# Linear attention and a highway layer on one core: a new order for the first chunk, with batch 1's query scaled on GpSimd

## The chip, the core and the metric

The kernel runs on one core of a Trainium2 chip. A core has five engines that work side by side, each with its own queue of instructions in program order: PE (matrix products, with its weight loads shown apart as PEld), DVE (VectorE), ACT (ScalarE), POOL (GpSimd) and SP, which here only issues the DMAs. Engines wait for each other by semaphores. Matrix products go to PSUM, which has eight banks of 128 x 512 numbers of 4 bytes; the rest lives in SBUF, 128 partitions wide. The metric is the time of one execution in microseconds on the device; lower is better.

## The reference

Eight batches, eight heads, 576 rows of 64. Every head computes a linear attention, and a highway layer with two 512 x 512 weights follows:

```
q_s = exp(q) / sum over d of exp(q)
k_s = exp(k) / sum over rows of exp(k)
kv  = k_s^T v                    (64 x 64 for each head)
x   = q_s kv, the heads side by side: 4608 x 512
H   = max(x w_h, 0)
T   = 1 / (1 + exp(-(x w_t + b_t)))
out = T H + (1 - T) x
```

(The reference subtracts maxima before the exponentials; they cancel.) Inputs and output are in 32 bits. The kernel works in 16 bits inside, sums products in 32, and uses T H + (1 - T) x = x + T (H - x), with T from a tanh: T = (1 + tanh(z / 2)) / 2.

## The kernel before

**Layout.** A batch is loaded by three DMAs of 1152 KB (`load`, L84). Two heads share the 128 partitions, and each partition holds nine consecutive rows (index n) of four head pairs (index c). "Half a" of a batch is the two head pairs 2a and 2a+1. The load pool `ld` has three buffers for each of q, k and v; the two weights borrow one buffer of q and one of k (`load_weight`, L99). All DMAs are issued by SP, in program order.

**One batch**, by function:

- `exp_half` (L150): ACT takes the exponential of half of q or k, 32 bits to 16, 128x1152. Tiles `eq` and `ek`.
- `cast_v` (L160): half of v to 16 bits with a column of ones beside it, on POOL unless another engine is given.
- `q_sums` (L195, L199): DVE sums each row of 64 exponentials of a half (tile `r`), and `q_recip` (L204) takes the reciprocals of the batch.
- The query is scaled in place, in two parts (n from 0 to 4 and from 4 to 9): on DVE by `q_scale_v` (a small copy L210 and a product L212 each), or on POOL by `q_scale_p` (L216). Batches 0 and 1 use DVE, the others POOL.
- `q_trans` (L218): PE transposes the scaled query in three groups (4, 4 and 1 rows n) into PSUM (tile `pq`, L64), and DVE copies each to SBUF (tile `qsT`, L233).
- `kv_half` (L167): 36 small products k^T v of half a batch into the two `psk` banks; `kv_norm` (L183): DVE divides by the sums of k that the ones column gave (tiles `rz`, `kvn`).
- `x_pair` (L235): x, transposed, for half a batch and eight of the nine rows n, from `kvn` and `qsT`; three of the four results of a batch are copied to `xT` by ACT (L255), the last by DVE (L257). `x_left` (L259) does the ninth row (tile `x`, L270).

**The highway layer** works by chunks: chunk c is batch c's x without the ninth rows (chunks 8 and 9 are the ninth rows of all batches), and each has four output blocks ob of 128 columns. `gate(c, ob)` (L286) is four matmuls with w_t and a tanh on ACT in place in PSUM (tile `pt`, L291). `carry(c, ob)` (L294) is four matmuls with w_h (tile `ph`) and on DVE `dd` = max(ph, 0) - x (L300). `blend(c, ob)` (L305) is `g` = (tanh + 1) dd on DVE (L308). `out_tile` turns x and g back by matmuls (tile `nat`), and the result is stored.

**PSUM** is dealt to three pools: `ps_ht` with four banks (gates, carries and the warm-up tile), `ps_q` with three (`pq`, `psk`, `px`, `px_l`), `ps_nat` with one. A pool gives a new tile the free bank that was released longest ago, and its first writer waits until the readers of the old tile are done. A gate's bank is released by its blend, a carry's by its dd, the two `psk` banks by `kv_norm`.

**The order** is written out by hand, because the scheduler is switched off (L57). Each engine's queue is the order in which the code emits that engine's instructions. The list at L441 to L468 holds the head: all of batch 0's attention, chunk 0 of the highway layer, batch 1's attention, and the first steps of batch 2. Idle time of PE is filled there with `warm_up` matmuls whose result nobody reads. After it, events at slots p (L380) follow: chunk c has slots 8c to 8c+7, a gate and a carry in turn, and a blend two slots after its gate. A table (L426 to L430) puts batch b's transpositions, kv halves and x_pairs at offsets from slot p = 8(b - 1); `kv_norm` stands right behind the second kv half. For batch 2 the offsets are transpositions 4, 5, 5, kv halves 3, 4, x 6, 7, 7. Within a slot of this table the transpositions are emitted ahead of the kv half.

Loads of the head: q, k, v of batch 0 in halves, the bias, then q of batch 1, w_t, w_h, k of batch 1, v of batch 1 in halves. The loads of batches 2 and 3 stand in the head's list, later ones at slot 8(b - 3).

Of the kernel before, what the change touches and what calls it, by code (L numbers as in the profile page):

```python
# [18 lines left out]
def kernel(  # L19
# [19 lines left out]
    def heads_view(t, b):  # L39
        return t[b].rearrange("(c x) (p n) d -> (x p) c (n d)", x=2, n=N9)  # L40

    pool = lambda name, bufs, **kw: ctx.enter_context(tc.tile_pool(name=name, bufs=bufs, **kw))
    consts = pool("consts", 1)
    ld = pool("ld", 3)
    ekp = pool("ekp", 2)
    eqp = pool("eqp", 2)
    small = pool("small", 2)
# [1 line left out]
    xtp = pool("xtp", 3)  # L49
    gp = pool("gp", 2)  # L50
    mo = pool("mo", 3)
    og = pool("og", 3)
    ps_ht = pool("ps_ht", 4, space=PSUM)
    ps_q = pool("ps_q", 3, space=PSUM)
    ps_nat = pool("ps_nat", 1, space=PSUM)
# [3 lines left out]
    mm = lambda o, l, r, st, sp: nc.tensor.matmul(  # L59
        o, l, r, start=st, stop=sp, skip_group_check=True  # L60
    )
# [6 lines left out]

    ident = consts.tile([P, P], FP16, name="ident")
    half_i = consts.tile([P, P], FP16, name="half_i")  # L70
    w16 = {n: consts.tile([P, 4, 512], FP16, name=f"w16{n}") for n in "ht"}
    brow = consts.tile([4, P], FP32, name="brow")
    id4 = consts.tile([4, 4], FP32, name="id4")
    bt2 = consts.tile([P, 4], FP32, name="bt2")
    kvn = [consts.tile([P, 2, 2, 64], FP16, name=f"kvn{i}") for i in range(2)]
    v16s = [consts.tile([P, N9, 4, 66], FP16, name=f"v16_{i}") for i in range(2)]
    x9 = consts.tile([P, 4, B, 64], FP16, name="x9")
# [35 lines left out]
    for w in "qkv":  # L113
        load(0, w, [nc.sync, nc.sync])
    nc.sync.dma_start(brow, moe_b_t.rearrange("(k p) -> k p", p=P))
    load(1, "q")
    load_weight("t", moe_w_t, "q32")
    load_weight("h", moe_w_h, "k32")
    load(1, "k")
    load(1, "v", [nc.sync, nc.sync])  # L120
# [18 lines left out]
    wide = consts.tile([P, 512], FP16, name="wide")  # L139
    nc.vector.memset(wide, 0.0)  # L140

    def warm_up(n):
        for _ in range(n):
            mm(warm, ident, wide, True, True)


    ek, eq, psk, qsT = {}, {}, {}, {}
    xT, gT = {}, {}

    def exp_half(b, which, a):  # L150
        dst, p_ = {"k": (ek, ekp), "q": (eq, eqp)}[which]
        if a == 0:
            dst[b] = p_.tile([P, N9, 4, 64], FP16, tag="e", name=f"e{which}_{b}")
        nc.scalar.activation(  # L154
# [3 lines left out]
        )  # L158

    def cast_v(b, a, eng=None):  # L160
        (eng or nc.gpsimd).tensor_copy(  # L161
            v16s[b % 2][:, :, 2 * a : 2 * a + 2, 0:64],
            in32["v"][b][:, 2 * a : 2 * a + 2].rearrange("p c n d -> p n c d"),
        )


    def kv_half(b, a):  # L167
# [25 lines left out]
    qsum = {}  # L193

    def q_sums(b, a):  # L195
        if a == 0:
            qsum[b] = small.tile([P, N9, 4], FP32, tag="r32", name=f"r32_{b}")
        h = slice(2 * a, 2 * a + 2)
        nc.vector.reduce_sum(qsum[b][:, :, h], eq[b][:, :, h, :], axis=AX.X)  # L199

    NG = [(0, 4), (4, 8), (8, 9)]

# [70 lines left out]
    rows_of = lambda c: 8 if c < B else 4  # L273

    def views(c):
        if c >= B:
            h = slice(4 * (c - B), 4 * (c - B) + 4)
            return lambda k_: x9[:, k_, h], lambda k_: g9[:, k_, h]
        g, b2 = c // 2, c % 2
        if g not in gT:  # L280
            gT[g] = gp.tile([P, 4, NM, 2, 64], FP16, tag="g", name=f"g_{g}")
        return lambda k_: xT[g][:, k_, :, b2, :], lambda k_: gT[g][:, k_, :, b2, :]

    live = {}

    def gate(c, ob):  # L286
        xv = views(c)[0]
        ps = ps_ht.tile([P, rows_of(c), 64], FP32, tag="ht", name=f"pt_{c}_{ob}")
        for k_ in range(4):
            mm(ps, w16["t"][:, k_, ob * P : ob * P + P], xv(k_), k_ == 0, k_ == 3)  # L290
        nc.scalar.activation(ps, ps, AF.Tanh, bias=bt2[:, ob : ob + 1], scale=0.5)  # L291
        live[c, ob] = ps
# [101 lines left out]
    for g in range(B // 2):  # L394
        p = 16 * (g + 1)
# [6 lines left out]
    p = 8 * B + 8  # L402
# [5 lines left out]
    at(9, E(exp_half, 2, "k", 0), E(q_scale_p, 2, 4, N9))  # L408
    at(10, E(exp_half, 2, "k", 1))
    at(11, E(cast_v, 2, 1, nc.vector))  # L410
    for b in range(2, B):
        p = 8 * (b - 1)
        if b > 2:
            s = p + {3: -2, 4: -4}.get(b, -5)
            at(s, E(exp_half, b, "q", 0))
            at(s + 1, E(exp_half, b, "q", 1), E(q_sums, b, 0))
            at(s + 2, E(q_sums, b, 1), E(q_recip, b))
            if b > 3:
                at(s + 2, E(q_scale_p, b, 0, 4))
# [10 lines left out]
        }.get(b, ((2, 3, 4), (3, 4), (5, 6, 7)))  # L430
# [10 lines left out]
    for f in [  # L441
        E(warm_up, 20),
        E(exp_half, 0, "q", 0), E(q_sums, 0, 0),
        E(exp_half, 0, "q", 1), E(q_sums, 0, 1),
        E(q_recip, 0), E(q_scale_v, 0, 0, 4), E(q_scale_v, 0, 4, N9),
        E(exp_half, 0, "k", 0), E(cast_v, 0, 0),
        E(exp_half, 0, "k", 1), E(cast_v, 0, 1),
        E(q_trans, 0, 0), E(q_trans, 0, 1), E(warm_up, 2), E(q_trans, 0, 2),
        E(warm_up, 6),
        E(kv_half, 0, 0), E(gate_bias), E(warm_up, 2), E(kv_half, 0, 1), E(kv_norm, 0),  # L450
        E(warm_up, 4),
        E(x_pair, 0, 0), E(warm_up, 2), E(x_pair, 0, 1), E(warm_up, 2), E(x_left, 0),
        E(warm_up, 14),
        E(exp_half, 1, "q", 0), E(exp_half, 1, "q", 1),
        E(q_sums, 1, 0),
        *[E(cast_weight, "t", k_, nc.vector) for k_ in range(4)],
        E(q_sums, 1, 1), E(q_recip, 1), E(q_scale_v, 1, 0, 4), E(q_scale_v, 1, 4, N9),
        *[E(cast_weight, "h", k_, (nc.gpsimd, nc.scalar)[k_ % 2]) for k_ in range(4)],
        E(gate, 0, 0), E(gate, 0, 1), E(exp_half, 1, "k", 0), E(cast_v, 1, 0),
        E(carry, 0, 0), E(blend, 0, 0), E(carry, 0, 1), E(blend, 0, 1),  # L460
        E(exp_half, 1, "k", 1), E(cast_v, 1, 1),
        E(q_trans, 1, 0), E(q_trans, 1, 1), E(q_trans, 1, 2),
        E(gate, 0, 2), E(carry, 0, 2), E(blend, 0, 2),
        E(kv_half, 1, 0), E(gate, 0, 3), E(kv_half, 1, 1), E(kv_norm, 1),
        E(carry, 0, 3), *[E(load, b, w) for b in (2, 3) for w in "qkv"],
        E(exp_half, 2, "q", 0),
        E(x_pair, 1, 0), E(x_pair, 1, 1), E(blend, 0, 3), E(x_left, 1),
        E(exp_half, 2, "q", 1), E(q_sums, 2, 0),  # L468
    ]:
        f()  # L470
    for p in range(8, 8 * (B + 2) + 1):
# [33 lines left out]
```

The softmax here doesn't subtract the row's maximum and nothing guards it: scores larger than these inputs give would overflow.

## Time and profile before

| What | Value |
|---|---|
| median of 4 runs (lowest, highest) | 140.39 us (140.24, 140.57) |
| the profiled execution | 140.24 us |
| its span, first to last instruction | 138.2 us |
| granted PE clock, mean | 0.996 |
| busy: PE, PEld | 122.4 us (89%), 69.4 us (50%) |
| busy: DVE, ACT, POOL | 107.1 us (78%), 88.6 us (64%), 44.3 us (32%) |
| DMA | 40.07 MB, mean 290 GB/s |

The profile's second part cuts the span into 40 slices of 3.455 us; a digit is the busy share in tenths:

```
PE   4979999967978799969979999899899999999950
DVE  1395289987998799996998789988987766688860
ACT  3650376819931998639978969769793645565430
POOL 2006003410393619039409800980394000000000
DMA  4999999999999999943999999970043007066774
```

PE's busy time counts the warm-up matmuls of the first 21 us, and matmuls are pipelined, so a 9 is not PE at its best. The DMA engines are full up to about 58 us. Of the chain of work that ended last, PE has 50% of the span, DVE 31%, ACT and POOL 5% each, DMA 3%. Some moments of the head: ACT starts on batch 0's query at 4.41 us, batch 0's products x end near 18, chunk 0's first dd starts at 24.94, batch 1's first x_pair at 31.82, the gate of slot 8 at 34.17, batch 2's first x_pair at 44.37.

A row of the timeline reads: start, duration (both in us), engine, line, operation, output and inputs, shapes, count; in brackets the idle time of that engine just before and what ended it.

### The profile page before, as it was taken

The numbers are of one execution on the slowest core, as the hardware profiler recorded it, in microseconds if no ns is written. First come the engines' busy times: TensorE is split into PE (matmuls) and PEld (weight loads), VectorE is DVE, ScalarE is ACT, GpSimd is POOL, SyncE is SP. The second block draws the span as 40 slices with busy tenths as digits, with TensorE's granted clock in tenths as the row PEclk, the third lists the DMA queues.
The fourth block names the chain that finished last, engine by engine and source line by source line (L and its number), as shares of the span: only waits on it lengthen the run. The fifth ranks groups of instructions, "written<-read, shape, count | busy, mean of one in ns | idle before, by whom it ended". The sixth has DMA issues, their size and how long they took to land.

```text
span 138.2 us, 3619 instructions
## 1 busy us (share of the span) xinstructions
PE 122.4 (89%) x1509; PEld 69.4 (50%) x1509; DVE 107.1 (78%) x208; ACT 88.6 (64%) x130; POOL 44.3 (32%) x37
## 2 busy tenths in 40 slices
PE   4979999967978799969979999899899999999950
PEld 1335344532443355526634654465366455699930
DVE  1395289987998799996998789988987766688860
ACT  3650376819931998639978969769793645565430
POOL 2006003410393619039409800980394000000000
PEclk9999999999999999999999999999999999999998
DMA  4999999999999999943999999970043007066774
GB/s 140 375 386 411 401 389 413 409 413 403 414 414 398 413 409 410 406 176 152 277 409 408 319 312 406 397 294 0 5 175 130 5 0 304 0 251 277 292 267 136
DMA packets 15783, 40.07 MB, mean 290 GB/s; under 512 B 660, under 2 KB 1176, under 8 KB 14744
## 3 DMA queue, kind: packets, MB, share of 16 engines
q1 hardware_dynamic: 15768, 39.85, 75.1%
q8 instruction: 12, 0.20, 0.5%
q14 instruction: 3, 0.02, 0.1%
HBM read 30.41 MB, written 9.44 MB: 288 GB/s over the span
## 4 chain that ended last, share of the span: by engine, by line
PE 50%; DVE 31%; ACT 5%; POOL 5%; issue 3%; DMA 3%; DVEq 0%; POOLq 0%
PE pt L59 14%; DVE r L199 13%; PE ph L59 13%; PE nat L59 9%; POOL eq L216 5%; PE pq L64 4%; DVE g L308 4%; PE psk L59 3%; DVE dd L300 3%; PE warm L59 3%; DMA q<-in_q_dram 3%; ACT eq L154 2%; DVE eq L212 2%; PE px L59 2%; DVE r L204 2%
## 5 line engine op out<-in xcount | busy, mean ns | idle before, releaser
L291 ACT ACTIVATE pt<-pt,bt 128x512 f32<-128x512 f32 (+1 forms) x40 | 24.8, 622 | 27.4 <-PE pt L59 27.4
L59 PE MATMUL pt<-xT,w16t 128*128 128x512 f16 x128 | 33.3, 380 | 2.2 <-DVE xT L257 1.7
L216 POOL TENSOR_TENSOR eq<-eq,r 128x1024 f16<-128x1024 f16 (+1 forms) x12 | 25.6, 2152 | 29.5 <-DVE r L204 29.5
L59 PE MATMUL ph<-xT,w16h 128*128 128x512 f16 x128 | 32.8, 380 | 0.0
L300 DVE SCALAR_TENSOR_TENSOR dd<-ph,xT 128x512 f16<-128x512 f32 x32 | 21.8, 682 | 7.5 <-PE ph L59 7.5
L308 DVE SCALAR_TENSOR_TENSOR g<-pt,dd 128x512 f16<-128x512 f32 (+1 forms) x40 | 25.2, 630 | 2.4
L199 DVE TENSOR_REDUCE r<-eq 128x18 f32<-128x1152 f16 x16 | 21.4, 1344 | 4.2 <-ACT eq L154 4.2
L161 POOL CAST v<-v 128x1152 f16<-128x1152 f32 x15 | 16.9, 1147 | 22.9 <-DMA v<-in_v_dram 20.7
L154 ACT ACTIVATE eq<-q 128x1152 f16<-128x1152 f32 x16 | 18.5, 1172 | 2.6 <-DMA q<-in_q_dram 2.6
L59 PEld LDWEIGHTS <-w16t 128*128 128x128 f16 x160 | 14.0, 97 | 12.3 <-issue 1.1
L59 PE MATMUL nat<-half_i,g 128*128 128x128 f16 x142 | 19.8, 219 | 0.1
L154 ACT ACTIVATE ek<-k 128x1152 f16<-128x1152 f32 x16 | 18.4, 1169 | 1.9 <-DMA k<-in_k_dram 1.9
L59 PEld LDWEIGHTS <-w16h 128*128 128x128 f16 x160 | 13.8, 98 | 10.9 <-issue 1.4
L339 ACT COPY o<-nat 128x512 f32<-128x512 f32 x28 | 16.6, 593 | 2.8 <-PE nat L59 2.0
L59 PE MATMUL nat<-ident,xT 128*128 128x128 f16 x128 | 17.7, 219 | 0.0
L255 ACT CAST xT<-px 128x512 f16<-128x512 f32 x24 | 13.3, 592 | 6.5 <-PE px L59 6.4
L59 PE MATMUL warm<-wide,ident 128*128 128x512 f16 x52 | 15.2, 441 | 1.9 <-DVE wide L140 1.9
L59 PEld LDWEIGHTS <-g 128*128 128x128 f16 x144 | 14.0, 98 | 3.5 <-DVE g L308 0.6
L233 DVE COPY qsT<-pq 128x1024 f16<-128x1024 f16 (+1 forms) x24 | 12.8, 553 | 3.2 <-PE pq L64 3.0
L59 PEld LDWEIGHTS <-xT 128*128 128x128 f16 x128 | 12.5, 98 | 5.0 <-issue 2.6
L64 PE MATMUL pq<-ident,eq 128*128 128x128 f16 x144 | 11.5, 220 | 2.5 <-POOL eq L216 1.4
L64 PEld LDWEIGHTS <-eq 128*128 128x128 f16 x144 | 8.9, 98 | 6.4 <-POOL eq L216 3.1
(43 smaller groups left out, 86.4 us busy)
## 6 DMA issues: line engine op xcount, KB each, us to landing
out_dram<-o SPq DMA_DIRECT2D x8, 1024.0 KB, 4.6
q<-in_q_dram SPq DMA_DIRECT2D x7, 1152.0 KB, 13.8
k<-in_k_dram SPq DMA_DIRECT2D x7, 1152.0 KB, 14.8
v<-in_v_dram SPq DMA_DIRECT2D x6, 1152.0 KB, 14.7
v<-in_v_dram SPq DMA_DIRECT2D x4, 576.0 KB, 10.7
q<-in_q_dram SPq DMA_DIRECT2D x2, 576.0 KB, 4.1
k<-in_k_dram SPq DMA_DIRECT2D x2, 576.0 KB, 6.8
w32t<-in_moe_w_t_dram SPq DMA_DIRECT2D x1, 1024.0 KB, 13.2
```

Source lines behind the costliest of these rows:

```text
L59: mm = lambda o, l, r, st, sp: nc.tensor.matmul(o, l, r, start=st, stop=sp, skip_group_check=True)
L64: nc.tensor.matmul(o, i, ident, is_transpose=True, start=True, stop=True, skip_group_check=True,)
L154: nc.scalar.activation(dst[b][:, :, 2 * a : 2 * a + 2, :], in32[which][b][:, 2 * a : 2 * a + 2].rearrange("p c n d -> p n c d"), AF.Exp,)
L161: (eng or nc.gpsimd).tensor_copy(v16s[b % 2][:, :, 2 * a : 2 * a + 2, 0:64], in32["v"][b][:, 2 * a : 2 * a + 2].rearrange("p c n d -> p n ...
L199: nc.vector.reduce_sum(qsum[b][:, :, h], eq[b][:, :, h, :], axis=AX.X)
L216: nc.gpsimd.tensor_mul(e, e, r.broadcast_to(list(e.shape)))
L233: nc.vector.tensor_copy(qsT[b][:, :, n0:n1, :], t[:, :, 0:w, :])
L255: nc.scalar.copy(dst, t[c])
L291: nc.scalar.activation(ps, ps, AF.Tanh, bias=bt2[:, ob : ob + 1], scale=0.5)
L300: nc.vector.scalar_tensor_tensor(dd, ps, 0.0, xv(ob), op0=ALU.max, op1=ALU.subtract)
L308: nc.vector.scalar_tensor_tensor(gv(ob), th, 1.0, dd, op0=ALU.add, op1=ALU.mult)
L339: nc.scalar.copy(o, flat(t))
```

## The change

- Loads: w_t moves ahead of batch 1's query. Batch 2's v is loaded in two halves. The load of batches 2 and 3 stands at another place of the list.
- w_t's four casts stand ahead of batch 0's x_pair and go to DVE and POOL in turn, instead of four on DVE behind it. w_h's casts stay on POOL and ACT in turn.
- The fourteen warm-up matmuls behind batch 0's products go, and one more; five are put behind the third gate of chunk 0, in a bank of `ps_q`.
- Chunk 0's gates are computed before the carries: (0,0) and (0,1) in `ps_ht`, (0,2) in a bank of `ps_q`, and (0,3) in the bank of `ps_nat`, behind the second carry.
- Batch 1's query: ACT does its second half behind the tanh of gate (0,0); the sums are made by two additions and a reduction of a quarter of the length (`q_sums_tree`); the scaling is on POOL (`q_scale_p`) instead of DVE (`q_scale_v`), behind w_h's casts there.
- Batch 1's v: the first half is cast by ACT, the second as two single head pairs by POOL and ACT.
- Batch 1's transpositions, kv halves and the last blend of chunk 0 are put in another order; both exponentials of batch 2's query stand behind all of batch 1's x products.
- Batch 2's kv halves move from slots p+3 and p+4 to p+4 and p+5, `kv_norm` with the second.
- In SBUF a pad of 128 bytes, the load pool and the output pool now lie ahead of the constants.

```diff
+    pool("pad", 1).tile([P, PAD // 4], FP32, name="pad")
+    ld = pool("ld", 3)
+    og = pool("og", 3)
     consts = pool("consts", 1)
-    ld = pool("ld", 3)
...
+    load_weight("t", moe_w_t, "q32")
     load(1, "q")
-    load_weight("t", moe_w_t, "q32")
     load_weight("h", moe_w_h, "k32")
...
+    def warm_mid(n):
+        t = ps_q.tile([P, 512], FP32, tag="qx", name="warm_mid")
+        for _ in range(n):
+            mm(t, ident, wide, True, True)
...
+    def cast_v_head(b, c, eng):
+        o = v16s[b % 2][:, :, c, 0:64]
+        i = in32["v"][b][:, c]
+        if eng is nc.scalar:
+            eng.copy(o, i)
+        else:
+            eng.tensor_copy(o, i)
...
+    def q_sums_tree(b, a):
+        if a == 0:
+            qsum[b] = small.tile([P, N9, 4], FP32, tag="r32", name=f"r32_{b}")
+        h = slice(2 * a, 2 * a + 2)
+        e = eq[b][:, :, h, :]
+        nc.vector.tensor_add(t32, e[:, :, :, 0:32], e[:, :, :, 32:64])
+        nc.vector.tensor_add(t16, t32[:, :, :, 0:16], t32[:, :, :, 16:32])
+        nc.vector.reduce_sum(qsum[b][:, :, h], t16, axis=AX.X)
...
-    def gate(c, ob):
+    def gate(c, ob, home=None):
         xv = views(c)[0]
-        ps = ps_ht.tile([P, rows_of(c), 64], FP32, tag="ht", name=f"pt_{c}_{ob}")
+        ps, tag = home or (ps_ht, "ht")
+        ps = ps.tile([P, rows_of(c), 64], FP32, tag=tag, name=f"pt_{c}_{ob}")
...
-            2: ((4, 5, 5), (3, 4), (6, 7, 7)),
+            2: ((4, 5, 5), (4, 5), (6, 7, 7)),
...
+        *[E(cast_weight, "t", k_, (nc.vector, nc.gpsimd)[k_ % 2]) for k_ in range(4)],
         E(warm_up, 4),
-        E(x_pair, 0, 0), E(warm_up, 2), E(x_pair, 0, 1), E(warm_up, 2), E(x_left, 0),
-        E(warm_up, 14),
-        E(exp_half, 1, "q", 0), E(exp_half, 1, "q", 1),
-        E(q_sums, 1, 0),
-        *[E(cast_weight, "t", k_, nc.vector) for k_ in range(4)],
-        E(q_sums, 1, 1), E(q_recip, 1), E(q_scale_v, 1, 0, 4), E(q_scale_v, 1, 4, N9),
+        E(x_pair, 0, 0), E(warm_up, 2), E(x_pair, 0, 1), E(warm_up, 1), E(x_left, 0),
+        E(exp_half, 1, "q", 0), E(q_sums_tree, 1, 0),
+        E(gate, 0, 0), E(exp_half, 1, "q", 1), E(q_sums_tree, 1, 1), E(q_recip, 1),
         *[E(cast_weight, "h", k_, (nc.gpsimd, nc.scalar)[k_ % 2]) for k_ in range(4)],
-        E(gate, 0, 0), E(gate, 0, 1), E(exp_half, 1, "k", 0), E(cast_v, 1, 0),
-        E(carry, 0, 0), E(blend, 0, 0), E(carry, 0, 1), E(blend, 0, 1),
-        E(exp_half, 1, "k", 1), E(cast_v, 1, 1),
-        E(q_trans, 1, 0), E(q_trans, 1, 1), E(q_trans, 1, 2),
-        E(gate, 0, 2), E(carry, 0, 2), E(blend, 0, 2),
-        E(kv_half, 1, 0), E(gate, 0, 3), E(kv_half, 1, 1), E(kv_norm, 1),
-        E(carry, 0, 3), *[E(load, b, w) for b in (2, 3) for w in "qkv"],
-        E(exp_half, 2, "q", 0),
-        E(x_pair, 1, 0), E(x_pair, 1, 1), E(blend, 0, 3), E(x_left, 1),
-        E(exp_half, 2, "q", 1), E(q_sums, 2, 0),
+        E(q_scale_p, 1, 0, 4), E(q_scale_p, 1, 4, N9),
+        E(gate, 0, 1), E(gate, 0, 2, (ps_q, "qx")), E(warm_mid, 5),
+        E(carry, 0, 0), E(blend, 0, 0), E(carry, 0, 1), E(exp_half, 1, "k", 0),
+        E(gate, 0, 3, (ps_nat, "nat")), E(blend, 0, 1), E(carry, 0, 2),
+        E(q_trans, 1, 0), E(carry, 0, 3), E(blend, 0, 2),
+        E(exp_half, 1, "k", 1), E(cast_v, 1, 0, nc.scalar),
+        E(cast_v_head, 1, 2, nc.gpsimd), E(cast_v_head, 1, 3, nc.scalar),
+        E(q_trans, 1, 1), E(kv_half, 1, 0), E(q_trans, 1, 2), E(kv_half, 1, 1),
+        E(kv_norm, 1), E(blend, 0, 3),
+        *[E(load, 2, w) for w in "qk"], E(load, 2, "v", [nc.sync, nc.sync]),
+        *[E(load, 3, w) for w in "qkv"],
+        E(x_pair, 1, 0), E(x_pair, 1, 1), E(x_left, 1),
+        E(exp_half, 2, "q", 0), E(exp_half, 2, "q", 1), E(q_sums, 2, 0),
```

More of the change, by code (lines that the diff above doesn't have):

```diff
@@ L32 @@
     P = 128
+    PAD = 128
     N9 = S // 64
@@ L51 @@
     mo = pool("mo", 3)
-    og = pool("og", 3)
     ps_ht = pool("ps_ht", 4, space=PSUM)
@@ L160, in cast_v @@
     def cast_v(b, a, eng=None):
[L161 to L164, printed above, removed]
+        o = v16s[b % 2][:, :, 2 * a : 2 * a + 2, 0:64]
+        i = in32["v"][b][:, 2 * a : 2 * a + 2].rearrange("p c n d -> p n c d")
+        if eng is nc.scalar:
+            eng.copy(o, i)
+        else:
+            (eng or nc.gpsimd).tensor_copy(o, i)
+    def cast_v_head(b, c, eng):
+        o = v16s[b % 2][:, :, c, 0:64]
+        i = in32["v"][b][:, c]
+        if eng is nc.scalar:
+            eng.copy(o, i)
+        else:
+            eng.tensor_copy(o, i)
     def kv_half(b, a):
@@ L199, in q_sums @@
         nc.vector.reduce_sum(qsum[b][:, :, h], eq[b][:, :, h, :], axis=AX.X)
+    t32 = consts.tile([P, N9, 2, 32], FP16, name="t32")
+    t16 = consts.tile([P, N9, 2, 16], FP16, name="t16")
+    def q_sums_tree(b, a):
[6 more added lines that the diff above has]
+        nc.vector.reduce_sum(qsum[b][:, :, h], t16, axis=AX.X)
     NG = [(0, 4), (4, 8), (8, 9)]
```

## The prediction

> **What bounds the kernel now.** The profiled execution took 140.24 us, of which 138.2 are the span and 2.04 lie around it; the median shown is 140.39, 0.15 more. I work in span times and add 2.04. The table of stretches came first: does an early gain survive to the end?
>
> ```profile
> 34.20:47.30 13.10, 10.77 (x141) 5.11 (x138) 11.76 (x23) 7.75 (x11) 8.02 (x5) 1.00 1.04 409
> 47.30:62.00 14.70, 13.06 (x170) 7.00 (x167) 13.98 (x25) 11.19 (x16) 5.32 (x3) 1.00 0.92 359
> 74.20:87.00 12.80, 12.66 (x173) 7.12 (x172) 10.81 (x21) 10.79 (x16) 5.59 (x5) 1.00 0.99 358
> 112.00:121.00 9.00, 9.00 (x76) 5.58 (x75) 5.68 (x10) 5.18 (x10) 0.00 (x0) 1.00 0.28 117
> ```
>
> Columns: stretch, length, busy time of PE, weight load, DVE, ACT, POOL, granted clock, DMA share, GB/s. From 47.3 DVE is nearly full (13.98 of 14.70), from 74 PE is (12.66 of 12.80), and the code there is untouched. Loads do not bind there: SP issues batch 5's three loads between 41 and 47 us, and between 59 and 66 us the DMA row falls to 4 and 3 tenths. So whatever is won or lost by the first half of batch 2's products (x_pair, 44.37 us) reaches the end one for one. The whole question is when that instruction runs.
>
> Ahead of it I read the timeline for the arrivals, which no edit can pull forward:
>
> ```profile
> 21.44 1.14 ACT L109 CAST w16h<-w32h 128x512 f16<-128x512 f32 x2 [1.66 <-DMA w32h<-in_moe_w_h_dram]
> 21.47 1.17 POOL L111 CAST w16h<-w32h 128x512 f16<-128x512 f32 x2 [7.96 <-DMA w32h<-in_moe_w_h_dram]
> 24.25 2.22 ACT L154 ACTIVATE ek<-k 128x1152 f16<-128x1152 f32 x2 [0.53 <-DMA k<-in_k_dram]
> 27.16 1.15 POOL L161 CAST v<-v 128x1152 f16<-128x1152 f32 x1 [0.27 <-DMA v<-in_v_dram]
> 35.88 1.15 POOL L161 CAST v<-v 128x1152 f16<-128x1152 f32 x1 [7.57 <-DMA v<-in_v_dram]
> ```
>
> Bracketed: idle time and what ended it. w_h's cast, batch 1's k and v, and batch 2's v wait on memory while DMA runs at 1.04 and 409 to 412 GB/s. DVE, though, is late at the first carry, and the batch 2 query later waits for POOL:
>
> ```profile
> 24.20 0.82 DVE L212 TENSOR_TENSOR eq<-eq,r 128x1280 f16<-128x1280 f16 x1
> 24.94 0.68 DVE L300 SCALAR_TENSOR_TENSOR dd<-ph,xT 128x512 f16<-128x512 f32 x1
> 25.73 0.69 DVE L308 SCALAR_TENSOR_TENSOR g<-pt,dd 128x512 f16<-128x512 f32 x1
> ...
> 38.15 4.64 POOL L216 TENSOR_TENSOR eq<-eq,r 128x1024 f16<-128x1024 f16 x2 [1.12 <-DVE r L204]
> 38.60 1.02 PE L59 MATMUL pt<-xT,w16t 128*128 128x512 f16 x4 [0.40 <-DVE dd L300]
> 42.84 0.56 PEld L64 LDWEIGHTS <-eq 128*128 128x128 f16 x10 [1.10 <-POOL eq L216]
> ```
>
> The first carry's sum (ready on PE near 23.6) waits behind DVE's scaling of q1 until 24.94. The 38.60 row also shows how banks are handed on: gate (1,2) waits for a dd, the reader of the bank released longest ago. I use that order below.
>
> **The change, step by step.**
>
> *Landings.* Issue start plus time to landing: q1 4.20+11.0=15.2, w_t 4.63+13.2=17.83, w_h 5.77+15.6=21.37. Swapped, w_t lands 2.63 after v0 (cast starts 12.37): 15.0, and q1 at 17.8, where ACT is free anyway (17.66). w_h trails by 3.54 although w_t, of equal size, took 2.63; k1 (2.81) and q2 (2.84), larger, took less too. I take 20.6, near the usual spacing; bounds 20.46 and 21.37.
>
> *Removed.* Fourteen warm-up matmuls (17.9 to 21) and one more; the gates (0,0) to (0,2) and five matmuls take their place. Cost nothing: the clock stayed 1.00 across PE's own holes in 24.94 to 31.8 (5.46 busy of 6.86). w_t's casts: two on DVE (0.36 apart) between 15.40 and x_pair's copy at 17.11, two on POOL (0.59 each): hidden; a landing past 16.4 would push that copy.
>
> *q1's sums.* Per half two adds and a short reduction for one reduction of 1.34. From the fp16 products (1024: 0.69, 1280: 0.825, so 0.52 ns an element) the adds of 576 and 288 cost 0.46 and 0.31; the reduction of 288 lies between 0.16 (DVE's smallest row) and 1.34, at its rate 0.44. With two waits of 0.1: 1.4, no gain. Exponentials at 17.9 and 19.6 with a tanh between, sums to 22.2, reciprocal to 22.6.
>
> *q1's scaling to POOL.* Leaves DVE (0.18+0.69+0.18+0.83); POOL's rows for the same shapes are 1.90 and 2.40, together 4.30 (4.18 to 4.64 pair by pair): 22.75 to 27.05. Its second transposition is then ready at 27.7; DVE reaches its copy at 27.9 (below). Cover 0.2; past it each POOL microsecond is on the path. [...]
>
> *First chunk.* In the trace w_h's landing to the end of both casts is 1.27 (21.37 to 22.64); the last two matmuls with weights (0.10+0.22+0.22) and their fill bring dd to landing plus 2.07: 22.67 instead of 24.94. From there DVE is back to back: a dd to its own blend 0.79, other steps 0.61, a large copy 0.60. dd 22.67, g 23.46, dd 24.07, g 24.86, dd 25.47, query copy 26.07, dd 26.67, g 27.28, query copy 27.88 to 28.57. All four gates are done before that, in banks of the three PSUM pools; the tanh behind the w_h casts on ACT (to 23.7) are early enough for these g.
>
> The third, short transposition gets the bank of the second (two are held by kv): PE 28.62, ready 28.90. The second kv half stands behind it and needs v: ACT does k's exponentials (to 27.05), v's first half (shape not in the trace: between 0.615, a 512 cast, and 1.17, the exponential of 1152; I take 1.17) and one head (0.65), to 28.75. So kv 28.8 to 29.28, normalisation 0.69, x_pair(1,0) at 30.17 instead of 31.82: minus 1.65.
>
> *Query of batch 2.* Its two exponentials now both follow x_pair's three ACT copies (0.54 apart, from 30.62): 32.24 and 33.31, the second ending 34.47 (before 35.0). Sums from 33.45 two times 1.27, reciprocal 36.05, POOL 0.53 behind as in the trace: 36.58, before 38.15. v2's cast stands ahead on POOL: its first half lands 1.45 before 35.75, at 34.3, cast to 35.45, hidden; unsplit it would end at 36.9 and cost 0.3. The halves of v1 (25.74, 27.16, behind k1 at 24.18) together take the 2.9 of a whole load, so the split costs the queue nothing. [...] Scaling ends at E = 36.58+4.30 = 40.88 (before 42.80).
>
> *kv of batch 2, two slots later.* This gives back. Its halves now hold two of ps_q's three banks while both last transpositions run through the third. From E: transposition 0.66, copy to 1.38, third transposition 1.43 to 1.71, kv half (behind it on PE) to 2.05, short copy to 2.03, normalisation 2.09 to 2.78, x_pair at E+2.93; before E+1.57 (42.80 to 44.37). So 43.81: minus 0.56. The gate, dd and tanh queued behind on PE and ACT move with it. The placement of buffers: no row depends on an address; loads into three different buffers all take 2.8 to 2.9; I take 0.
>
> **Sum:** 140.24 - 0.56 = **139.7** (139.8 beside the median).
>
> **Rivals.**
> A, forecast: 139.7. With the bounds (w_h 20.46, POOL 4.18; x_pair(1,0) is held at 30.1 by v's casts): E 40.68, 139.5. 42 in 100, 138.9 to 139.95.
> B, the turn through one bank is hidden, by kv being ready and DVE free: E+1.57 = 42.45, minus 1.9, 138.3. For it: PE sits idle ahead of E. Against it: two banks held are two banks held. 16 in 100.
> C, no change: w_h lands at 21.37 as before. dd 23.44, x_pair(1,0) 30.88, POOL 37.3, E 41.6, x_pair(2,0) 44.53: 140.4. The landing row speaks for it, the other spacings against. 17 in 100.
> D, slower: the one-bank turn outweighs the head. It decides once E is past 41.44 (44.37 less 2.93); with w_h at 21.37 and POOL at its slow 4.64 (the row of 38.15, while DVE casts v) E is 41.93, x_pair 44.86: 140.7; with q1's POOL scaling past its 0.2 of cover, up to 141. 25 in 100.
>
> Under 0.2% (0.28 us) a measurement cannot tell from no change. Faster: A and B, 0.58; same: C, 0.17; slower: D, 0.25. Range 138.2 to 141.0; A's own is 139.5 to 139.95.
>
> **What would show it.** First dd near 22.7 (23.4 is C or D); x_pair(1,0) near 30.2; POOL's batch 2 scaling from 36.6; x_pair(2,0) 2.9 behind its end and not 1.6. If the slices after 62 shift by another amount than x_pair(2,0), or DVE or clock rows change there, the one-for-one step is wrong. A slower clock before 31, or landings that move beyond q1 and w_t, would break the head.

## The result and the profile after

| | before | after |
|---|---|---|
| median, runs | 140.41 us, 60 runs | 143.93 us, 37 runs |
| lowest, highest | 139.93, 145.04 | 140.33, 146.01 |
| profiled execution, its span | 140.24, 138.2 us | 140.53, 138.7 us |
| granted PE clock in it | 0.996 | 0.987 |

The change made the kernel slower: the ratio to the kernel before is 1.0034, 95% interval 1.002 to 1.0048, about 0.5 us; this ratio leaves out runs more than 1.5% above the fastest of their kernel. The changed kernel's times fall in two groups: 14 runs from 140.33 to 141.76, with granted clocks of 0.982 to 0.999, and 23 from 143.25 to 146.01, with 0.942 to 0.964. The profiled run belongs to the lower group. Of the kernel before, 4 runs of 60 lie at 143 or more. So the 0.5 us is the loss of the lower group; the median of all 37 runs is 3.5 us above that of the kernel before.

Marks of the two profiles, in us (line numbers below are the changed kernel's):

| mark | before | forecast | after |
|---|---|---|---|
| w_t landed | 17.83 | 15.0 | 15.17 |
| batch 1's q landed | 15.2 | 17.8 | 18.0 |
| w_h landed | 21.37 | 20.6 | 21.65 |
| first dd | 24.94 | 22.67 | 23.74 |
| x_pair(1,0) | 31.82 | 30.17 | 30.88 |
| reciprocal of batch 2 | 37.62 | 36.05 | 36.92 |
| POOL scales batch 2: start, length | 38.15, 4.64 | 36.58, 4.30 | 37.45, 4.64 |
| E, its end | 42.80 | 40.88 | 42.09 |
| x_pair(2,0) | 44.37 | 43.81 | 45.12 |

The timeline of the changed kernel where w_h arrives:

```profile
21.71 1.14 ACT L112 CAST w16h<-w32h 128x512 f16<-128x512 f32 x2 [0.53 <-DMA w32h<-in_moe_w_h_dram]
21.74 1.30 POOL L114 CAST w16h<-w32h 128x512 f16<-128x512 f32 x2 [5.37 <-DMA w32h<-in_moe_w_h_dram]
...
22.53 0.38 DVE L235 RECIPROCAL r<-r 128x36 f32<-128x36 f32 x1
...
23.06 4.19 POOL L247 TENSOR_TENSOR eq<-eq,r 128x1024 f16<-128x1024 f16 x2
...
23.74 0.69 DVE L332 SCALAR_TENSOR_TENSOR dd<-ph,xT 128x512 f16<-128x512 f32 x1 [0.83 <-PE ph L62]
```

DVE is free from 22.91 and waits 0.83 for PE's carry, which waits for the casts, which wait for the load. Before, DVE was late there; now the load is. Still the head is 1.2 us earlier at the first dd. The same timeline at the turn of batch 2:

```profile
37.45 4.64 POOL L247 TENSOR_TENSOR eq<-eq,r 128x1024 f16<-128x1024 f16 x2 [0.99 <-DVE r L235]
...
39.15 0.87 DVE L174 CAST v<-v 128x1152 f16<-128x1152 f32 x1
...
42.14 0.62 PE L67 MATMUL pq<-ident,eq 128*128 128x128 f16 x8 [0.74 <-DVE dd L332]
42.80 0.69 DVE L264 COPY qsT<-pq 128x1024 f16<-128x1024 f16 x1 [0.67 <-PE pq L67]
43.54 0.27 PE L67 MATMUL pq<-ident,eq 128*128 128x128 f16 x2 [0.78 <-DVE qsT L264]
...
43.74 0.48 PE L62 MATMUL psk<-v,ek 64*64 64x65 f16 x36
43.85 0.29 DVE L264 COPY qsT<-pq 128x256 f16<-128x256 f16 x1 [0.36 <-PE pq L67]
...
44.28 0.24 DVE L204 RECIPROCAL rz<-psk 128x2 f32<-128x2 f32 x2
44.48 0.49 DVE L206 TENSOR_TENSOR kvn<-psk,rz 128x128 f16<-128x128 f32 x2
...
45.12 0.41 PE L62 MATMUL px<-qsT,kvn 64*64 64x512 f16 x4
```

PE and DVE hand each other one bank: PE fills it, DVE copies it (0.67 of waiting), PE may fill it again (0.78), and the second kv half and the normalisation stand behind. (The row of 42.14 names a dd that ended at 42.13; POOL had ended at 42.09.) Before, the second kv half was done ahead of E, and both transpositions ran as one:

```profile
42.85 0.73 PE L64 MATMUL pq<-ident,eq 128*128 128x128 f16 x10 [0.61 <-POOL eq L216]
...
44.37 0.41 PE L59 MATMUL px<-qsT,kvn 64*64 64x512 f16 x4
```

From E to x_pair(2,0) it is 3.03 us; before it was 1.57. That 1.46 takes back more than the 0.71 by which E is earlier. Behind it nothing changes. The table of stretches, its columns as before, starts each stretch 0.85 and then 0.75 us later:

```profile
35.05:48.05 13.00, 10.52 (x135) 4.82 (x133) 10.48 (x20) 7.19 (x11) 8.02 (x5) 0.96 1.04 409
48.05:62.75 14.70, 13.07 (x170) 7.00 (x167) 13.97 (x25) 11.20 (x16) 5.32 (x3) 1.00 0.86 339
74.95:87.75 12.80, 12.67 (x173) 7.12 (x172) 10.80 (x21) 10.79 (x16) 5.59 (x5) 1.00 0.99 355
112.75:121.75 9.00, 9.00 (x77) 5.56 (x75) 5.69 (x10) 5.17 (x10) 0.00 (x0) 1.00 0.28 117
```

DVE 13.97 against 13.98 of 14.70, PE 12.67 against 12.66 of 12.80: the same work, 0.75 later. Only in the last stores do 0.25 come back (span plus 0.5).

### The profile page after: what moved, and what is told of

Read it like the earlier page. It is cut to its first block, busy times and chain, and to the rows that moved or that the text cites. A ratio compares the mean times of both kernels' runs of the same rounds, so it can differ in the third digit from the quotient of the medians.

```text
span 138.7 us, 3595 instructions
## 1 busy us (share of the span) xinstructions
PE 120.8 (87%) x1499; PEld 68.9 (50%) x1499; DVE 105.4 (76%) x206; ACT 90.2 (65%) x132; POOL 48.2 (35%) x40
## 4 chain that ended last, share of the span: by engine, by line
PE 48%; DVE 25%; DMA 11%; SPq 4%; POOL 4%; ACT 3%; issue 3%; DVEq 0%; POOLq 0%
PE ph L62 14%; PE pt L62 14%; DMA w32h<-in_moe_w_h_dram 11%; DVE r L217 9%; PE nat L62 9%; PE pq L67 5%; DVE dd L332 5%; DVE g L340 4%; SPq L95 4%; PE psk L62 3%; POOL eq L247 3%; DVE qsT L264 2%; PE px L62 2%; DVE xT L288 2%; DVE r L235 1%
## 5 line engine op out<-in xcount | busy, mean ns | idle before, releaser
L247 POOL TENSOR_TENSOR eq<-eq,r 128x1024 f16<-128x1024 f16 (+1 forms) x14 | 29.8, 2148 | 29.9 <-DVE r L235 29.9
L62 PE MATMUL pt<-xT,w16t 128*128 128x512 f16 x128 | 34.0, 388 | 1.8 <-DVE xT L288 1.7
L62 PE MATMUL ph<-xT,w16h 128*128 128x512 f16 x128 | 33.4, 384 | 0.3 <-POOL w16h L114 0.3
L332 DVE SCALAR_TENSOR_TENSOR dd<-ph,xT 128x512 f16<-128x512 f32 x32 | 21.8, 682 | 8.5 <-PE ph L62 8.4
L217 DVE TENSOR_REDUCE r<-eq 128x18 f32<-128x1152 f16 x14 | 18.7, 1345 | 4.6 <-ACT eq L162 4.6
L174 POOL CAST v<-v 128x1152 f16<-128x1152 f32 x13 | 14.6, 1146 | 20.3 <-DMA v<-in_v_dram 17.2
L62 PE MATMUL warm<-wide,ident 128*128 128x512 f16 x37 | 10.8, 434 | 1.9 <-DVE wide L143 1.9
```

The costliest lines, as they stand in the source:

```text
L62: mm = lambda o, l, r, st, sp: nc.tensor.matmul(o, l, r, start=st, stop=sp, skip_group_check=True)
L174: (eng or nc.gpsimd).tensor_copy(o, i)
L247: nc.gpsimd.tensor_mul(e, e, r.broadcast_to(list(e.shape)))
L332: nc.vector.scalar_tensor_tensor(dd, ps, 0.0, xv(ob), op0=ALU.max, op1=ALU.subtract)
```

## The experiments

"Changed" is the changed kernel. x_pair(2,0), its distance from E and the span are of the profiled run, the ratio is to the kernel before, with its interval.

| run | ratio | median (range), runs | x_pair(2,0) | behind E | span |
|---|---|---|---|---|---|
| e1 changed, kv offsets 3, 4 | 0.9933 (0.9906 to 0.996) | 139.35 (138.87 to 141.71), 8 | 44.97 | 3.71 | 138.5 |
| e2 before, kv offsets 4, 5 | 1.0103 (1.009 to 1.0117) | 141.87 (141.64 to 145.87), 6 | 49.94 | 3.04 | 143.9 |
| e3 changed, q1 scaled on DVE | 1.032 (1.0289 to 1.0351) | 144.92 (143.78 to 145.53), 6 | 49.09 | 5.97 | 142.9 |
| e4 changed, v2's cast on ACT | 1.0009 (0.9988 to 1.0031) | 140.48 (139.97 to 142.12), 12 | 44.94 | 3.03 | 138.5 |
| e5 changed, PE kept busy | 1.0083 (1.005 to 1.0116) | 141.54 (140.85 to 142.54), 8 | 45.16 | 3.03 | 139.1 |
| e6 = e1 and e5 | 0.9941 (0.9918 to 0.9964) | 139.63 (139.13 to 140.39), 6 | 43.49 | 1.58 | 137.5 |
| e7 changed, w_h ahead of q1 | one run | 148.62 | 52.61 | 6.07 | 146.5 |
| e8 changed, old placement | none | 144.69 (141.5 to 146.84), 6 | 48.27 | 6.07 | 143.1 |
| e9 = e1 and e4 | 0.9934 (0.9904 to 0.9964) | 139.47 (138.4 to 140.27), 7 | 42.83 | 1.58 | 136.4 |
| e10 = e9, q2's exponential early | 0.9853 (0.981 to 0.9895) | 139.12 (137.59 to 139.89), 6 | 42.53 | 1.58 | 136.1 |
| e11 changed, v2's cast later | 1.0103 (1.0065 to 1.0141) | 142.85 (141.09 to 144.23), 10 | 46.59 | 4.95 | 141.1 |
| e12 changed, 4 warm-ups first | 1.0077 (1.0047 to 1.0107) | 141.91 (141.0 to 145.96), 8 | 49.11 | 6.20 | 143.8 |
| e13 changed, w_h not awaited | 1.0002 (0.9964 to 1.004) | 142.28 (139.44 to 144.84), 12 | 44.26 | 3.04 | 137.8 |
| e14 = e13 and e4 | 0.9989 (0.9961 to 1.0018) | 140.53 (139.43 to 141.38), 12 | 45.44 | 3.05 | 139.0 |

**The turn against the head (e1, e2).** My theory after the result was the forecast's rival D: the head gains, the one-bank turn takes more. The rival was that the head itself had gained nothing. The edit takes the kv offsets back in the changed kernel, and puts them alone into the kernel before.

```diff
-            2: ((4, 5, 5), (4, 5), (6, 7, 7)),
+            2: ((4, 5, 5), (3, 4), (6, 7, 7)),
```

> The changed kernel with batch 2's kv halves back at offsets 3 and 4. Theory (the turn through one bank costs the change its gain): the end of POOL's batch 2 scaling, E, stays near 42.1; the first x_pair of batch 2 comes 1.6 behind it instead of 3.0, at 43.7 instead of 45.1, and the time falls by 1.4, to 139.3 (0.992 to 0.993 of before). Rival (the later kv was needed, because at offset 3 PE would stand at a kv half whose k or v is not there, or because the head alone is slower): x_pair stays at 44.8 or later, 140.5 or more.

> The kernel before with batch 2's kv halves at offsets 4 and 5 and nothing else. Theory: E stays at 42.8, x_pair comes 3.0 behind it, at 45.8 instead of 44.4, and the time rises by 1.4, to 141.8 (1.010). Rival (the later kv costs only in the changed kernel, by its PSUM order or clock): within 0.3 of before.

Both times came as expected, and the four kernels make a square: the offsets cost 1.03% with the old head and 1.01% with the new (1.0034 - 0.9933), 1.4 us each; the new head gives 0.67% and 0.69%, 0.95 us. The two parts add up. e1's profiled run did not: it took 140.54, and its x_pair(2,0) came at 44.97, which was the rival's sign, because a cast on DVE took 2.95 us there (see the part on the cast below). The turn shows in other profiles, in the column "behind E": with offsets 4 and 5 it is 3.03 to 3.05 us wherever that cast did not come second (changed, e2, e4, e5, e13, e14), with 3 and 4 it is 1.57 or 1.58 (before, e6, e9, e10). e6 reads:

```profile
37.27 4.64 POOL L255 TENSOR_TENSOR eq<-eq,r 128x1024 f16<-128x1024 f16 x2 [1.46 <-DVE r L243]
...
43.49 0.41 PE L62 MATMUL px<-qsT,kvn 64*64 64x512 f16 x4
```

The profiled run of e2 had a mean clock of 0.978 (0.996 before), and its marks in batches 1 and 2 come some 4 us late (batch 2's reciprocal at 41.73, 37.62 before); the distance behind E is not touched by that.

**Scaling on POOL (e3).** In the changed kernel the scaling of batch 1's query goes back to DVE.

```diff
-        E(q_scale_p, 1, 0, 4), E(q_scale_p, 1, 4, N9),
+        E(q_scale_v, 1, 0, 4), E(q_scale_v, 1, 4, N9),
```

> The changed kernel with batch 1's query scaled on DVE again. Theory (DVE is the limit from the first dd to batch 1's x_pair): the scaling lies from 22.9 to 24.8, the first dd starts at 24.8 instead of 23.7, batch 1's first x_pair at 31.7 to 31.9 instead of 30.9, and the time rises by 0.7 to 1.0, to 141.5. Rival (POOL's scaling is what holds the head, by its 4.2 us): x_pair of batch 1 earlier than 30.9 and the time at or below 140.7.

The direction was right: x_pair(1,0) moved from 30.88 to 32.13. The median is 3.4 us above the expected 141.5. The profile shows two things that I had not counted: a clock of 0.50 between 33 and 39 us and again between 47 and 49, and DVE's cast of batch 2's v, 2.19 us long instead of 0.87. All six runs lie where the upper group of the changed kernel lies, so the price of the scaling alone can't be read from the times. The cast is the subject of the next experiments, the clock of those behind them.

**A cast and a product that take turns (e4, e9, e11).** In the changed kernel's profile DVE's cast of v2's second half starts at 39.15, just ahead of POOL's second product; the cast lasts 0.87 and POOL's pair 4.64. In e1's profile POOL was first:

```profile
37.07 4.19 POOL L247 TENSOR_TENSOR eq<-eq,r 128x1024 f16<-128x1024 f16 x2 [1.43 <-DVE r L235]
...
38.98 2.95 DVE L174 CAST v<-v 128x1152 f16<-128x1152 f32 x1
```

The pair lasts 4.19, and the same cast 2.95. In the five profiles that show POOL first (e1, e3, e8, e11, e12) the cast ends 0.67 to 0.69 behind POOL's pair. e4 and e9 move the cast to ACT, with the changed kernel's offsets and with the old ones; e11 leaves it on DVE, one slot later, so that POOL comes first.

```diff
-    at(11, E(cast_v, 2, 1, nc.vector))
+    at(11, E(cast_v, 2, 1, nc.scalar))    # e4, e9
+    at(12, E(cast_v, 2, 1, nc.vector))    # e11
```

> The changed kernel with the cast of the second half of batch 2's v on ACT instead of DVE. Theory (that DVE cast, which runs at the same time, is what makes POOL's pair of products last 4.64 instead of 4.19): the pair lasts 4.19, E is 0.45 earlier, and the time falls by 0.4 to 0.5, to 140.3; DVE also has 0.6 less to do ahead of the transposition's copy. Rival (the first pair is slow for another reason, loads for instance): the pair stays at 4.6 and the time within 0.2 of the changed kernel's.

> The changed kernel with both mended: batch 2's kv halves one slot earlier (offsets 3 and 4), and the second half of batch 2's value cast on ScalarE instead of VectorE. [...] Rival (the spread of the earlier runs has nothing to do with the cast): the median is that of offsets 3 and 4 alone, 139.35, with runs up to 141.7.

> The changed kernel, with VectorE's cast of the second half of batch 2's value one slot later, behind blend(1,1): it is issued near 39.8, when GpSimd's second product has run since about 39.0. [...] Rival (the long cast comes from the clock or from a load in flight): the cast lasts 0.87 here as well and the time is that of the changed kernel, mostly 140.3 to 141.

In e4 the pair lasted 4.19, none of 12 runs passed 142.12, and the gain over the changed kernel's lower group was 0.25% (0.35 us), a little less than expected; the two intervals overlap. E was only 0.18 earlier (41.91), since the reciprocal ahead of the pair came later (37.19 against 36.92; see the clock below). In e9 x_pair(2,0) came at 42.83 (expected 43.2) and no run passed 140.27, but the median, 139.47 (expected 138.8 to 139.1), is that of e1 (139.35), as the rival said. The gain shows only against the runs in which the cast comes second, as in e1's profiled run (x_pair(2,0) at 44.97). e11, the timeline:

```profile
37.45 4.19 POOL L247 TENSOR_TENSOR eq<-eq,r 128x1024 f16<-128x1024 f16 x2 [0.59 <-DVE r L235]
...
39.95 2.37 DVE L174 CAST v<-v 128x1152 f16<-128x1152 f32 x1
...
42.25 0.67 DVE L264 COPY qsT<-pq 128x1024 f16<-128x1024 f16 x1
...
46.59 0.64 PE L62 MATMUL px<-qsT,kvn 64*64 64x512 f16 x4
```

and its stretches:

```profile
41.00:45.00 4.00, 1.66 (x49) 1.08 (x48) 3.50 (x5) 0.00 (x0) 0.64 (x1) 1.00 1.04 404
45.00:49.00 4.00, 4.00 (x21) 1.07 (x19) 1.36 (x6) 2.30 (x4) 2.24 (x2) 0.57 1.04 411
```

The clock was 1.00 from 36 to 42 us, while the cast ran, so the low clock is not what makes it long. The cast holds DVE until POOL is done; the copy of the query behind it is 1.7 us late (42.25 against 40.54), so PE has work for only 1.66 of 4 us (2.48 in the changed kernel), and in the next 4 us it is granted 0.57 of its clock. x_pair(2,0) is 1.47 late, and the rest of the span 0.93 longer. I had expected a cast of 1.5 to 3 us that starts second, a pair of 4.19 and a median of 142.5 to 146: the median, 142.85, lies in that range, and three of ten runs are under 141.5. The times of the whole set point the same way: with the cast on ACT (e4, e9, e10, e14) none of 37 runs passed 142.2; with it on DVE in the changed kernel's place 23 of 37 did. The pair e13 and e14, which differ in this cast alone, has six of 12 runs at 143 or more and none of 12. e8 and e12 leave the cast where the changed kernel has it; their profiled runs took 145.13 and 145.67, the cast came second (2.95 and 2.81 us), x_pair(2,0) came 6.07 and 6.20 behind E, and the clock was 0.50 from 47 to 51. That the 23 runs lost this race is therefore likely, but not shown: no profile of the changed kernel caught one, and e5 below removes the upper group too, by another edit.

**The clock (e5, e6).** In the changed kernel PE has little to do once chunk 0 is finished, and its clock drops (low from about 32.6 to 36.0); the table of stretches for PE alone (length, busy, clock, DMA share, GB/s):

```profile
30.00:32.00 2.00, 0.89 (x41) 1.00 1.04 411
32.00:34.00 2.00, 1.50 (x13) 0.65 1.05 403
34.00:36.00 2.00, 2.00 (x6) 0.50 1.04 409
```

Ten warm-up matmuls between 28 and 33 us, into a bank of `ps_ht`, keep PE busy; e6 has the old offsets too.

```diff
+        E(q_trans, 1, 1), E(warm_late, 2), E(kv_half, 1, 0), E(warm_late, 1),
+        E(q_trans, 1, 2), E(kv_half, 1, 1), E(warm_late, 3),
...
+        E(x_pair, 1, 0), E(warm_late, 3), E(x_pair, 1, 1), E(warm_late, 1), E(x_left, 1),
```

> The changed kernel with ten more warm-up matmuls in PE's holes between 28 and 33 us (two, one, three, three, one). Theory (PE loses its clock there because the change took chunk 0's last gate and carry out of that stretch): the granted clock stays 1.00 from 31 to 37, where it was 0.50 for some 3.4 us, and batch 2's first gate takes 1.04 and not 1.89. In the profiled run of the changed kernel the slow stretch lay beside the sums on DVE, so E and x_pair of batch 2 stay (42.1, 45.1) and the time is 140.4 to 140.8; runs in which it lay worse improve. Rival (the clock falls for a reason that PE's own work does not touch): the clock is 0.5 in that stretch again.

> The same ten matmuls, with batch 2's kv halves at offsets 3 and 4. Theory (the two costs are separate): clock 1.00, x_pair of batch 2 about 1.6 behind E, at 43.7, time 138.8 to 139.1 (0.989 to 0.991 of before). Rival (the matmuls stand in the way of the x products that they lie between): 139.4 or more.

In e5 the drop is gone: batch 2's first gate took 1.04 us (1.89 in the changed kernel), the carry behind it 1.03 (1.46). Yet x_pair(2,0) came at 45.16, as without: in that stretch DVE's sums set the time and the slow matmuls lay beside them. The drop cost the changed kernel's profiled run nothing. It is not always free: in e4 (clock 0.65 over 30 to 32 us) and in e12 the x products of batch 1 already ran slow (x_pair(1,0) takes 1.05 and 1.06 us instead of 0.62), and the reciprocal came 6.5 us behind x_pair(1,0) instead of 6.04. And none of e5's eight runs passed 142.54, though its cast stays on DVE: keeping PE busy takes the upper group away as well. Whether those runs need the late cast, the low clock or both is open; in the profiles of e5 and e6 the cast was first (0.87 us). The medians of both are above what I expected, by 0.7 and 0.5 us over the upper ends. In the profiled runs that is not in the work: the last copy of a result starts 89.50 us behind x_pair(2,0) in both and 89.49 in the changed kernel; the end of the span is 4.44 and 4.51 behind that copy instead of 4.09, and in e5 2.35 us lie around the span instead of 1.83. Why is open.

**The landing of w_h (e7, e8, e12, e13, e14).** w_h landed 3.65 us behind q1, against 2.6 for w_t behind v0. First, is it w_h's own load, and is it the placement?

```diff
-    load(1, "q")
     load_weight("h", moe_w_h, "k32")
+    load(1, "q")
```

> The changed kernel with w_h loaded ahead of batch 1's query. It asks what makes w_h land 3.6 us behind the load ahead of it. If something slows the queue from 18 to 21.5 us, w_h lands at 17.8 (2.63 behind w_t) and the query then takes 3.6 or more. If it belongs to w_h's own load, w_h lands at 18.7 and the query 2.9 later. The time gets worse in both cases, by 1 to 3 us, since ACT casts w_h behind the query's exponentials: 142 to 144.

> The changed kernel with the buffers in SBUF where the kernel before has them (no pad, load pool behind the constants, output pool last). Theory (placement costs and brings nothing): landings and time as in the changed kernel, 140.5 to 140.9. Rival (the new placement is why the second half of batch 0's q landed at 6.2 instead of 5.75 and all else 0.2 to 0.3 later): it lands at 5.75 again, w_h at 21.4, and the time falls by 0.3 to 0.4.

In e7 w_h landed at 18.2, 2.9 behind w_t, and q1 at 22.55, 4.35 behind w_h. So it is not w_h's own load. The late one is the third load behind batch 0's v, whichever it is: w_h behind q1 here, q1 behind w_h in e7, and w_h right behind w_t in the kernel before (3.54). It takes 3.1 to 4.35 us in both kernels and in e1, e4, e7, e9 and e11, and lands at 21.2 to 22.6. The expected time was missed (148.62 in one run, clock 0.95). e8, with the load and output pools behind the constants again and without the pad, is inconclusive in its times, which spread from 141.5 to 146.84; but the new placement does not make the second half of batch 0's q late (the exponential starts at 6.24 in the changed kernel and at 5.68 to 5.87 in e1 and e9 to e12, which have the same placement), and with the old one w_h was late too: the first dd waits 0.83 for PE's carry and starts at 24.30 (23.74 in the changed kernel). So the placement is not the cause.

At 17 to 18 us the table of DMA queues shows a packet of instructions, the only one in that part of the span:

```profile
q8 instruction: 1, 0.02, 6.0%
```

That is 6% of 16 engines for 1 us, one engine for nearly all of it. If PE's place in its program sets its time, fewer warm-ups should move it out of w_h's way.

```diff
-        E(warm_up, 20),
+        E(warm_up, 4),
```

> The changed kernel with 4 instead of 20 warm-up matmuls at the very start, 32 fewer TensorE rows. Theory (a packet of the instruction queue that falls at 17 to 18 us, when TensorE has come to a certain row of its program, delays whichever load is in flight, here moe_w_h): the packet falls later, after 20.5, moe_w_h lands near 20.7 instead of 21.65, the first dd starts near 22.8 instead of 23.7, and x_pair(1,0) at about 30.0 instead of 30.9; the GpSimd pair ends at about 41.3 and the time is 0.4 to 0.9 below the changed kernel, unless the clock, with less work ahead of the first transposes, is low before 12 us and takes some of it back. Rival (moe_w_h is slow of itself, or the packet falls by the clock and not by rows): it lands at 21.5 to 21.8 and the time is that of the changed kernel.

The packet moved to 19 to 20, and w_h landed at 21.8 all the same. The time got worse: in the profile batch 0's part ran slow (six warm-ups in 2.38 us instead of 1.46, first product x at 17.39 instead of 16.01), and the cast on DVE came second. In e9 the packet fell at 16 to 17, before q1 had landed (17.5), and w_h was late too (21.25, 3.75 behind q1). So the packet was not shown to be the cause. What delays the load stays open.

What it is worth was measured. In e13 the fp16 w_h is cast from w_t's buffer, so nobody waits for w_h; e14 has v2's cast on ACT besides. Both leave out the true w_h, so their output is not the layer's: they are probes of the time only.

```diff
-        *[E(cast_weight, "h", k_, (nc.gpsimd, nc.scalar)[k_ % 2]) for k_ in range(4)],
+        *[E(cast_weight, "h", k_, (nc.gpsimd, nc.scalar)[k_ % 2], "t") for k_ in range(4)],
```

> The changed kernel; the fp16 copy of moe_w_h is cast from moe_w_t's buffer, which lands at 15.2, so nothing waits for moe_w_h (its load still runs, and the carry is computed with the other weight). The casts then start when their engines come to them: GpSimd by 20, ScalarE behind the second exponential of batch 1's query at about 21.2. Theory (the landing of moe_w_h, 1 us later than forecast, holds the head): first dd near 23.1 or earlier instead of 23.74, x_pair(1,0) at 30.1 to 30.4 instead of 30.88, where v's casts hold it, the end of the GpSimd pair near 41.5 and the time 0.4 to 0.7 below the changed kernel's, with the same spread up to 146. Rival (the head is held by VectorE's chain of sums, which ends with the reciprocal at 22.9, and by v's casts): x_pair(1,0) stays at 30.7 to 30.9 and the time at 140.4 to 141 where it is not spread.

> The same, and the second half of batch 2's value is cast on ScalarE, so that the GpSimd pair lasts 4.19. Both terms that the forecast had too small are then at or below its values. Theory (the forecast's steps were right apart from these two): x_pair(1,0) at 30.1 to 30.4, GpSimd's pair from about 36.9 to 41.1, x_pair(2,0) 3.0 later at 44.1, a little before the 44.37 of the kernel before; median 139.4 to 140.0, that is 0.5 to 1.0 below the run with the cast alone on ScalarE (140.48), and the forecast of 139.7 holds. Rival (the head was oversold in other places as well): x_pair(2,0) not before 44.6 and the median 140.2 or more.

e13, the timeline:

```profile
30.02 0.62 PE L62 MATMUL px<-qsT,kvn 64*64 64x512 f16 x5 [0.61 <-DVE kvn L206]
...
36.06 0.38 DVE L235 RECIPROCAL r<-r 128x36 f32<-128x36 f32 x1
...
36.58 4.64 POOL L247 TENSOR_TENSOR eq<-eq,r 128x1024 f16<-128x1024 f16 x2 [1.21 <-DVE r L235]
...
44.26 0.41 PE L62 MATMUL px<-qsT,kvn 64*64 64x512 f16 x4
```

The forecast had 30.17, 36.05, 36.58 for the first three. Without the wait for w_h these marks are what was forecast, and the time of the runs in the ratio is that of the kernel before (1.0002; six of the 12 runs lie at 143 or more). e14 I had expected at 139.4 to 140.0. Its median is 140.53 and its x_pair(2,0) came at 45.44, which are the rival's signs; six runs lie at 139.43 to 140.31 and six at 140.75 to 141.38. The profiled run is of the second six, and there the clock was 0.50 between 12 and 15 us, so that x_pair(1,0) came at 31.64; from there to x_pair(2,0) it is 13.80 us, against 14.24 in e13. So the shorter pair is seen (0.44), but that the whole sum comes to 139.7 is not shown.

**A faster version (e10).** With the cast on ACT and the old offsets, x_pair(2,0) waits for batch 2's sums. ACT stands idle before x_pair(1,0) while the query lies in memory.

```diff
-        E(x_pair, 1, 0), E(x_pair, 1, 1), E(x_left, 1),
-        E(exp_half, 2, "q", 0), E(exp_half, 2, "q", 1), E(q_sums, 2, 0),
+        E(exp_half, 2, "q", 0), E(x_pair, 1, 0),
+        E(q_sums, 2, 0), E(x_pair, 1, 1), E(x_left, 1), E(exp_half, 2, "q", 1),
```

> The same as the run before it in this call, and batch 2's first query exponential is placed ahead of x_pair(1,0) (ScalarE is idle from 28.9 to 31.5, the query lies in memory from 30.2), its sums behind x_pair(1,0). Theory (what sets the rest is the end of the GpSimd pair of batch 2, and the pair waits for the sums): the second sums end near 35.6 instead of 36.9, the reciprocal near 36.0, GpSimd has v2's first cast until 36.4 and then the pair until about 40.6, x_pair(2,0) starts near 42.2, 1 us before that of the other run, and the time is 0.5 to 1.0 lower: 138.0 to 138.4. Rival (batch 2's own query is no longer what ends last, because the batch 1 gates and carries ahead of the x_pair on TensorE set its place): x_pair(2,0) stays within 0.3 of the other run, and so does the time.

```profile
30.01 1.16 ACT L162 ACTIVATE eq<-q 128x1152 f16<-128x1152 f32 x1 [0.62 <-DMA q<-in_q_dram]
...
31.46 0.62 PE L62 MATMUL px<-qsT,kvn 64*64 64x512 f16 x5 [0.61 <-DVE kvn L206]
...
34.85 1.35 DVE L217 TENSOR_REDUCE r<-eq 128x18 f32<-128x1152 f16 x1 [0.40 <-ACT eq L162]
```

From x_pair(1,0) to x_pair(2,0) it is 11.07 us (31.46 to 42.53) against 12.34 in e9 (30.49 to 42.83): 1.27 gained. In this profiled run 0.97 of it was lost ahead, where the clock was 0.52 between 12 and 15 us, so x_pair(2,0) is only 0.30 earlier than in e9, not the 1 us expected, and the median of all runs, 139.12, is 0.35 below e9's. Against both kernels the gain is clear: the highest of the six runs, 139.89, lies below the lowest of either (139.93 and 140.33), and the ratio is 0.9853 (0.981 to 0.9895).

## Why the prediction was wrong, step by step

- **What sets the end.** Confirmed. The last copy of a result starts 89.48 to 89.50 us behind x_pair(2,0) in both kernels and in e1, e2, e4, e5, e6, e9, e10, e13 and e14, for starts from 42.53 to 49.94. Where the clock was low behind it (e3, e7, e8, e11, e12) it is 89.76 to 90.59. What varies is the last store behind that copy: 4.34 us to the end of the span before and 4.09 in the changed kernel. This 0.25 was not in the forecast.
- **The landings: the step that failed.** w_t (15.17) and q1 (18.0) landed as forecast; w_h was taken at 20.6, "near the usual spacing", and landed at 21.65, behind even the bound of 21.37. The row of before, 3.54 for w_h, was the better guide than the shorter spacings of other loads. The step behind it was right: dd came 2.09 behind the landing (2.07 forecast). e13 prices the error: the POOL pair starts at 36.58 without the wait and at 37.45 with it, 0.87 us.
- **The sums of q1, its scaling on POOL, chunk 0, the query of batch 2.** Right: 0.46, 0.31 and 0.45 for the tree (estimated 0.46, 0.31, 0.44), 4.19 for the POOL pair (4.30), and in e13 x_pair(1,0), the reciprocal and the start of the pair within 0.15. Part of that is luck: in e13 the first dd came at 22.89, 0.22 later than forecast though nobody waited for w_h, and from it to x_pair(1,0) it took 7.13 us instead of 7.50.
- **The POOL pair of batch 2.** Taken at 4.30, it lasted 4.64: 0.34. The row of 38.15 had shown 4.64 beside DVE's cast of v, and the forecast gave that value to rival D only. e4, e9 and e11 show the cast to be the cause.
- **The one-bank turn.** Right: E plus 2.93 forecast, 3.03 measured; 1.4 us by e1 and e2. (The heading of that step says two slots later; each kv half moves by one.)
- **The sum.** 0.87, 0.34 and 0.10 make 1.31, which is 45.12 less the forecast's 43.81. The gain of the head, 1.92 at E, shrank to 0.71, the turn's cost of 1.46 did not, and the sign turned. That is rival D, whose point of decision was E past 41.44 (measured 42.09) and whose time was 140.7; the ratio gives 140.9 for the lower group.
- **Not foreseen.** The clock was taken to stay at 1.00, because it had done so across PE's holes before. It did not: it was 0.50 in 33 to 36 us here, which cost this run nothing and some 0.5 us in e4 and e12. The group at 143 to 146, 23 of 37 runs, was in no rival. For these runs the forecast is 4 to 6 us short, and the cause is suggested, not shown.

## What to carry to other kernels

A gain ahead of a turn and a cost in it are subtracted from each other, so price both by the rows of the profile's own slow case, and ask what sign the sum has when the worst row holds; here the late load's own spacing and the slow POOL pair stood in the profile and decided. Before two more tiles are held across a hand-over, count the banks that are left: with one, PE and DVE waited for each other at each step here (0.67 and 0.78 us). Where the rows show that the operations of two engines hold each other up (here the cast took 0.87 us if it started first and up to 2.95 if second), order them so that the short operation can't come second, or move it to a third engine: with the cast moved to ACT none of 37 runs was in the upper group.

## What the runs showed of the hardware

- DVE's cast of v2's second half (128x1152, 32 to 16 bits) and POOL's pair of products on batch 2's query hold each other up. The cast takes 0.87 us if it starts ahead of POOL's second product (changed kernel, e5, e6), and the POOL pair then 4.64; with the cast on ACT (e4, e9) the pair takes 4.19. If POOL's product is first (e1, e3, e8, e11, e12), the cast takes 2.19 to 2.95, ends 0.67 to 0.69 behind POOL, and POOL's pair stays at 4.19. Each time the one that started second lost time; why, no run here shows.
- PE's clock halved in the changed kernel without a long gap: 0.89 busy of 2 us at 30 to 32, with no gap of PE above 0.66, was followed by 0.65 at 32 to 34 and 0.50 at 34 to 36. The drop lasted about 3.4 us (32.6 to 36.0). It comes in some runs and not in others: e11's profiled run, with 0.90 busy in the same 2 us, kept 1.00. Why is open; over 28 to 32 us PE was busier there, 2.41 us against 2.01.
- The third load behind batch 0's v lands 3.1 to 4.35 us behind its predecessor in each of the three orders seen (3.54 before, 3.65 in the changed kernel, 4.35 in e7), with an instruction packet at 16 to 20 us; the cause is open.
